# Attention and a feed-forward layer on one core: rows in parts of 256 and 320, and two PSUM banks used for more than one thing

## The chip, the cores and the metric

The kernel runs on 1 core of one Trainium2 chip. The metric is the device time of one execution in microseconds (us). Times of the kernel before: median 686.18 us of 3 runs (685.65 to 686.38). PE stands for TensorE, DVE for VectorE, ACT for ScalarE, SP for the engine that issues most DMAs.

## The reference

Shapes: 8 batches, 8 heads, 576 rows, head size 64, 32 memory slots, model width 512, inner width 2048, all in float32.

```python
a = exp(phi - max(phi, axis=2)); a = a / sum(a, axis=2)      # over the rows, per head
k_m = einsum('bhsm,bhsd->bhmd', a, k);  v_m = the same with v
scores = q @ k_m.T / sqrt(64);  attn = softmax(scores)       # over 32 memory slots
x = attn @ v_m                                               # 4608 x 512
out = silu(x @ w_in) @ w_out                                 # the feed-forward layer
```

The kernel never forms x: it multiplies v_m with w_in first (P, 256 x 2048 for a batch), and attn with P.

## The kernel before, in words

Every product that counts is made of parts: a float32 number is split into a high part, which a one-pass matmul takes as it is, and a low part, and three products (high x high, high x low, low x high) are summed.

A batch is a pass. Its 576 rows are held as two parts of 288: each is 256 rows and half of the 64 rows that are left over. The first layer (h = attn P, line 822 in passes 2 to 7, line 678 in batches 0 and 1) writes two PSUM banks, h, one tile of `[128, 2, 512]`, allocated anew each step. silu reads h (lines 836 and 838; 703 and 705 in batches 0 and 1): the 256 main rows go to gbuf, the 32 of the left-over rows to gleft.

A pass from 2 on has 16 steps (slots 0 to 15). In step s = 8 t + j PE first runs `ffn1s(b, t, j)`, 12 matmuls for the row half t and two chunks of 128 of the inner width; then `run(b, s)` puts in what the table of events holds for that step; then `st_step` of the step before, 21 matmuls of 256 columns into four banks sum 0 to 3 (line 861), which make the second layer in seven products in place of eight. For these, `forms` makes high and low parts of seven combinations: ACT rounds three (840), DVE makes four sums (841 to 845), ACT rounds these (850, the second rounding), DVE makes the low parts (851, 852). In steps 2 and 11 (4 and 11 in pass 2) DVE does the second rounding (847, 848) since ACT has an exponential to do, with a table load before and after it. Passes 1, 3, 5 and 7 end with four left steps (slots 16 to 19) for the left-over rows of two batches.

The work for batch n = b + 1 is put into pass b as events: `phi_max`, `phi_fold`, `phi_sub`, `phi_exp` (a); `e_mm` in two parts (k_m and v_m, lines 335 and 345), and behind its second part the division by the sums on DVE (353, 355) and the two normalised halves kvn on ACT (359) and DVE (361); `e_tr` (transposes); `s_all` (scores, line 382); then softmax; `s_back` and `s_low` (transposes back, copy ahi on ACT line 466, alo on DVE 471); and four blocks of P, `p_mm` (line 640): 16 small matmuls into the two banks bg, then ACT copies the high part (656) and DVE makes the low part (658). Block k (512 of the inner width) is needed by steps 2k, 2k + 1, 2k + 8 and 2k + 9 of its pass. A DVE instruction of an event other than P and s_all stands behind the last low part of the step's forms and of P.

The order on PE, and on ACT from batch 1 on, is that of the text. DVE's order is the scheduler's, except for such ties. bg, two banks, serves P, e, its transposes and the scores; the scores' last 64 columns go beside h, in columns from 288 on of its banks. A tile is emptied before PE writes it anew.

Of the kernel before, what the change touches and what calls it, by code (L numbers as in the profile page):

```python
# [48 lines left out]
def attn_ffn_kernel(  # L49
# [166 lines left out]
    def beside_h(w):  # L216

        return [live["h"][:, i, HALF : HALF + w] for i in range(2)]
# [24 lines left out]
    def load_q(b, hf, few=False):  # L243
        t = sb.tile([P, NR, HALF], F32, tag=f"q{hf}", name=f"q{b}_{hf}", bufs=1)
        at[b]["q", hf] = t
        load(t.rearrange("p r s -> p (r s)"), qT[b, hf], few)
# [78 lines left out]
    def e_mm(b, cs=range(FULLC)):  # L325
        e, er, kvt, kr = (at[b][k] for k in ("e", "er", "kv", "kr"))
        if cs[0] == 0:
            at[b]["pt"] = beside_h(KVW) if b == 2 else banks(b)
# [34 lines left out]
    def e_tr(b):  # L363
        pt = beside_h(P) if b <= 2 else banks(b)
# [7 lines left out]
    def s_all(b):  # L372

        sc = at[b]["sc"] = sb.tile([P, 2, S], F32, tag="x" if b == 2 else "y", name=f"sc{b}", bufs=1)
        bg, left = bgtile(), beside_h(S - 512)
        kvT = at[b]["kvT"]
        w = 512 - HALF
        for hf, f, n in ((0, 0, HALF), (1, 0, w), (1, w, HALF - w)):
            for r in range(NR):
                for p in range(2):  # L380
                    to = left[p] if f else bg[:, p, hf * HALF : hf * HALF + n]
# [4 lines left out]
                        start=True, stop=True, skip_group_check=True,  # L386
# [7 lines left out]
    def s_mm(b, hf):  # L394
# [56 lines left out]
    def s_back(b, u):  # L451
# [13 lines left out]
        for x in ((0, HALF), (HALF, S)) if b == 1 else ((0, w),):  # L465
# [33 lines left out]
    def f_scores(u):  # L499
        if u == 0:  # L500
            t = [ps.tile([P, 512], F32, tag="acc", name=f"firsts{p}", bufs=NI) for p in range(2)]
        else:
            h = ps.tile([P, 2, 512], F32, tag="h", name="firsts", bufs=1)
            t = [h[:, p] for p in range(2)]
        kvT, q = at[0]["kvT"], at[0]["q", u]
        for r in range(NR):
            for p in range(2):
                nc.tensor.matmul(
                    t[p][M * r : M * (r + 1), :HALF],
# [4 lines left out]
        first["st", u] = t if u == 0 else h  # L514

    def f_copy(u):
# [3 lines left out]
        left = first["left"].rearrange("p (g h f) -> p g h f", g=2, h=2)[:, :, u]  # L520
        st = first["st", u]
        if u:
            nc.scalar.copy(t, st[:, :, : 2 * P])
            nc.scalar.copy(left, st[:, :, 2 * P : HALF])
            return
        nc.scalar.copy(t[:, 0], st[0][:, : 2 * P])
        nc.vector.tensor_copy(t[:, 1], st[1][:, : 2 * P])
        for p in range(2):
            nc.scalar.copy(left[:, p], st[p][:, 2 * P : HALF])

    def f_turn(u):
# [3 lines left out]
        else:  # L535
            t = ps.tile([P, 2, 512], F32, tag="h", name="firstu", bufs=1).rearrange("p b f -> p (b f)")
# [48 lines left out]
    def f_back(u):  # L585
# [27 lines left out]
    ALL, FIRST, SECOND = (0, S), (0, HALF), (HALF, S)  # L613
# [49 lines left out]
    def ffn1(b, fc, h=None, low_last=False):  # L663
# [4 lines left out]
        if h is None:  # L668
            h = live["h"] = ps.tile([P, 2, 512], F32, tag="h", name="h", bufs=1)
# [161 lines left out]
    def forms(b, t, j, h):  # L831
# [3 lines left out]
        w = MAIN // 2  # L835
# [31 lines left out]
    sums, begun = [], set()  # L867
    HIGH, LOW = ((0, 0), (0, 1)), ((1, 0),)

    def st_step(b, t, j, part):  # L870
        if j == 0:
            sums[:] = [ps.tile([P, DMODEL], F32, tag="acc", name=f"sum{i}", bufs=NI) for i in range(4)]
# [9 lines left out]
        order = [(HIGH, todo), (LOW, todo)]  # L882
        if j == NP - 1:
# [77 lines left out]
    def steady(b, n):  # L961
# [26 lines left out]
        for k in range(2):  # L988
            ev(b, 13 + k, p_mm, n, k * JW, JW)
# [10 lines left out]
    for b in range(B):  # L1000
# [11 lines left out]
        else:  # L1012
            ev(b, 0, win_load, b, 3)
            ev(b, 0 if b > 2 else 1, p_mm, b, 2 * JW, JW)
# [4 lines left out]
            ev(b, 2, p_mm, b, 3 * JW, JW)  # L1019
# [58 lines left out]
    idle = ps.tile([P, 2, 512], F32, tag="h", name="idle", bufs=1)[:, 0]  # L1078
# [230 lines left out]
```

## Time and profile before

| | |
|---|---|
| profiled execution | 686.28 us |
| its span | 684.4 us |
| median of the runs | 686.18 us |
| PE busy | 673.4 us (98%) |
| DVE busy | 515.2 us (75%) |
| ACT busy | 368.0 us (54%) |
| granted clock | 1.000 (mean), 9 in each of 40 slices |
| first-layer matmuls of the passes | 1152 of 128x288 |

Busy times add up what an engine works on, and a matmul's row runs from its issue to its modelled end, so rows of PE overlap and the distance between starts tells what PE can do. In a timeline, a row's bracket is the idle time of the engine before it and what ended it.

### The profile page before, as it was taken

What the parts mean: (1) busy time and instruction counts of PE and PEld (TensorE: products, weight loads), DVE (VectorE), ACT (ScalarE), POOL (GpSimd) and SP (SyncE); (2) the same over time, 40 slices, a digit from 0 to 9 for tenths busy, and PEclk for the clock granted to TensorE, in tenths of its full rate; (3) what the DMA queues carried; (4) which work ended last, traced back from release to release, by engine and by line L of the source; (5) the groups of instructions that cost most, each with busy time, mean ns of one, the idle gap of its engine ahead of it and who ended that gap; (6) DMA issues with size and microseconds to landing.
All of it is one profiled execution on the core that took longest, in us unless ns stands there. A gap on an engine that the chain in (4) does not pass through costs nothing.

```text
span 684.4 us, 14813 instructions
## 1 busy us (share of the span) xinstructions
PE 673.4 (98%) x5932; PEld 595.5 (87%) x5932; DVE 515.2 (75%) x1085; ACT 368.0 (54%) x677; POOL 0.7 (0%) x6
## 2 busy tenths in 40 slices
PE   8999999999999999999999999999999999999997
PEld 3578777887889998899998999899989999889997
DVE  4897899788938588868876678786885668767653
ACT  3778684533625455654644546563653646554541
POOL 0000000000000000000000000000000000000000
PEclk9999999999999999999999999999999999999999
DMA  9988984224260462253420444235431204210001
GB/s 341 338 337 278 314 317 158 105 110 148 92 222 16 151 226 85 78 169 138 171 93 17 139 132 181 73 94 182 154 105 52 79 1 155 82 58 17 32 1 47
DMA packets 38228, 93.93 MB, mean 137 GB/s; under 512 B 4752, under 2 KB 22032, under 8 KB 34576
## 3 DMA queue, kind: packets, MB, share of 16 engines
q1 hardware_dynamic: 37136, 90.22, 38.0%
q10 hardware_dynamic: 1024, 2.77, 1.1%
q8 instruction: 47, 0.77, 0.4%
q14 instruction: 21, 0.17, 0.1%
HBM read 77.22 MB, written 15.73 MB: 136 GB/s over the span
## 4 chain that ended last, share of the span: by engine, by line
PE 77%; DVE 5%; ACT 2%; issue 1%; DMA 1%; SPq 0%; DVEq 0%; ACTq 0%
PE sum L861 32%; PE h L822 20%; PE acc L719 7%; PE lsum L861 5%; PE h L678 4%; PE bg L640 4%; PE accleft L719 2%; PE bg L335 1%; PE bg L382 1%; DMA fm<-fm 1%; ACT gbuf L836 1%; DVE gbuf L841 0%; DVE pm L658 0%; DVE sc L431 0%; DVE smx L427 0%
## 5 line engine op out<-in xcount | busy, mean ns | idle before, releaser
L822 PE MATMUL h<-aparts,pm 128*128 128x288 f32 x1152 | 168.8, 295 | 0.2 <-ACT gleft L838 0.2
L822 PEld LDWEIGHTS h<-aparts,pm 128*128 128x128 f32 x1152 | 157.0, 188 | 0.8 <-ACT gleft L838 0.5
L836 ACT ACTIVATE gbuf<-h 128x512 f32<-128x512 f32 x96 | 57.3, 596 | 122.5 <-PE h L822 120.5
L861 PE MATMUL sum<-wo_hi,aparts 128*128 128x256 f32 x384 | 103.9, 293 | 0.0
L861 PE MATMUL sum<-kept,aparts 128*128 128x256 f32 x576 | 100.1, 282 | 0.0
L861 PE MATMUL sum<-wo_lo,aparts 128*128 128x256 f32 x384 | 100.0, 282 | 0.0
L841 DVE TENSOR_TENSOR gbuf<-gbuf 128x256 f32<-128x256 f32 x96 | 40.5, 422 | 76.1 <-ACT gbuf L836 75.5
L861 PEld LDWEIGHTS sum<-wo_hi,aparts 128*128 128x128 f32 x384 | 72.7, 189 | 19.2 <-ACT gleft L838 16.7
L850 ACT ACTIVATE aparts<-gbuf 128x512 fp32r<-128x512 f32 x86 | 54.4, 633 | 65.2 <-DVE gbuf L845 65.2
L719 PE MATMUL acc<-wo_hi,gparts 128*128 128x512 f32 x256 | 86.5, 397 | 0.4 <-DVE gparts L695 0.3
L861 PEld LDWEIGHTS sum<-kept,aparts 128*128 128x128 f32 x576 | 82.5, 191 | 0.0
L852 DVE TENSOR_TENSOR gparts<-gbuf,aparts 128x512 fp32r<-128x512 f32 x86 | 59.5, 692 | 19.2 <-ACT aparts L850 19.2
L861 PE MATMUL sum<-wo_hi,gparts 128*128 128x256 f32 x384 | 73.2, 281 | 0.0
L861 PEld LDWEIGHTS sum<-wo_lo,aparts 128*128 128x128 f32 x384 | 73.1, 190 | 0.0
L861 PE MATMUL sum<-kept,gparts 128*128 128x256 f32 x288 | 65.5, 282 | 0.0
L719 PEld LDWEIGHTS acc<-wo_hi,gparts 128*128 128x128 f32 x256 | 47.7, 188 | 14.7 <-DVE gparts L695 1.8
L861 PEld LDWEIGHTS sum<-wo_hi,gparts 128*128 128x128 f32 x384 | 59.4, 190 | 0.0
L678 PEld LDWEIGHTS h<-aparts,pm 128*128 128x128 f32 x372 | 51.8, 188 | 6.7 <-issue 2.7
L678 PE MATMUL h<-aparts,pm 128*128 128x288 f32 x372 | 56.0, 299 | 0.5 <-ACT aparts L608 0.4
L719 PE MATMUL acc<-wo_lo,gparts 128*128 128x512 f32 x128 | 50.5, 394 | 0.8 <-DVE wo_lo L184 0.7
L840 ACT ACTIVATE aparts<-gbuf 128x384 fp32r<-128x384 f32 x96 | 50.4, 525 | 0.0
L861 PEld LDWEIGHTS sum<-kept,gparts 128*128 128x128 f32 x288 | 47.9, 190 | 0.0
(206 smaller groups left out, 986.3 us busy)
## 6 DMA issues: line engine op xcount, KB each, us to landing
win<-win_saved SPq DMA_DIRECT2D x24, 1024.0 KB, 4.9
kv<-in_kv SPq DMA_DIRECT2D x28, 516.0 KB, 4.7
q<-in_q SPq DMA_DIRECT2D x16, 576.0 KB, 5.4
raw<-in_w_in SPq DMA_DIRECT2D x14, 512.0 KB, 7.3
raw<-in_w_out SPq DMA_DIRECT2D x6, 1024.0 KB, 5.9
win_saved<-win SPq DMA_DIRECT2D x4, 1024.0 KB, 9.0
phi<-in_phi SPq DMA_DIRECT2D x7, 576.0 KB, 5.8
out<-oo SPq DMA_DIRECT2D x26, 128.0 KB, 1.8
```

What stands on the lines that cost most here:

```text
L335: nc.tensor.matmul(pt[p][M * r : M * (r + 1), :KVW], e[:, p, c, M * r : M * (r + 1)], kvt[c][:, p, r], start=c == 0, stop=False, skip_grou ...
L382: nc.tensor.matmul(to[M * r : M * (r + 1)], kvT[D * p : D * (p + 1), 0, r], at[b]["q", hf][D * p : D * (p + 1), r, f : f + n], start=True, ...
L640: nc.tensor.matmul(bg[M * r : M * (r + 1), p, :w].rearrange("p (k f) -> p k f", f=P), kvT[D * p : D * (p + 1), 1, r], src[D * p : D * (p + ...
L678: nc.tensor.matmul(h[:, hf, :HALF], wt[:, p, fs], a[:, p, hf * HALF : (hf + 1) * HALF], start=n[hf] == 0, stop=n[hf] == 5, skip_group_chec ...
L719: nc.tensor.matmul(acc[key], gt[:, cs], wt[:, fc], start=fc == 0 and n == 0, stop=fc == NFC - 1 and n == 2)
L822: nc.tensor.matmul(h[:, i, :HALF], wt[:, p, f : f + P], a[:, p], start=n == 0, stop=n == 5)
L836: nc.scalar.activation(gbuf[:, :MAIN].rearrange("p (i f) -> p i f", i=2), h[:, :, :w], AF.Silu)
L840: nc.scalar.activation(hi[:, :3], g[:, 1:4], AF.Copy)
L841: nc.vector.tensor_tensor(g[:, 4:6], g[:, :1].broadcast_to([P, 2, P]), g[:, 1:3], op=ALU.subtract)
L850: nc.scalar.activation(hi[:, 3:], g[:, 4:], AF.Copy)
L852: last_split.append(nc.vector.tensor_tensor(lo[:, 3:], g[:, 4:], hi[:, 3:], op=ALU.subtract))
L861: nc.tensor.matmul(sums[bank][:, place * Q : (place + 1) * Q], gt[:, k], wt, start=bank not in begun, stop=True, skip_group_check=True,)
```

## The change

The rows of a batch are held as parts of 256 and 320 rows; the 64 left-over rows are all in the second. h becomes two tiles of one bank each. In passes from 2 on they are allocated once: in the first half (steps 0 to 7) both chunks of 256 columns stand in h[0], and h[1] is free; in the second half each chunk of 320 columns has a bank. The four sums are also allocated once; each uses its whole bank but sum 3, which uses 256 of 512 columns. For n > 2, e's two halves go to h[1] and the free half of sum 3's bank; for n > 3 the transposes go to h[1], and the scores' left-over columns to h[1] and sum 3's bank. In some steps the three matmuls on sum 3 come last. e's DVE instructions in passes 3 and later are no longer tied behind the low parts.

Blocks of P: P(2) of a pass moves from step 0 to 3 (pass 2: 1 to 2), P(3) from step 2 to 5, pass 7 stays. So in passes 3 to 6 P(2) stands in front of e's first part and P(3) in front of its second. P(0) of the next batch moves from step 13 to 12 in pass 2; in passes 3 and 5 P(0) and P(1) move from steps 13 and 14 to slot 17, one behind the other, P(1) into h and P(0) into bg. silu reads bank by bank; in the head, the scores of the second part are copied by ACT and DVE, and turned into bg.

```diff
+CUT = MAIN // 2
+PART = ((0, CUT), (CUT, S))
+WIDE = S - CUT
...
     def e_mm(b, cs=range(FULLC)):
         if cs[0] == 0:
-            at[b]["pt"] = beside_h(KVW) if b == 2 else banks(b)
+            if b > 2:
+                at[b]["pt"] = spare_bank()[:, :KVW], accs()[3][:, Q : Q + KVW]
+            else:
+                at[b]["pt"] = beside_h(KVW) if b == 2 else banks(b)
...
     def e_tr(b):
-        pt = beside_h(P) if b <= 2 else banks(b)
+        if b > 3:
+            pt = [spare_bank()[:, k * P : (k + 1) * P] for k in range(2)]
+        else:
+            pt = beside_h(P) if b <= 2 else banks(b)
...
     def s_all(b):
-        bg, left = bgtile(), beside_h(S - 512)
+        bg = bgtile()
+        left = [spare_bank()[:, :LEFT], accs()[3][:, Q + KVW : Q + KVW + LEFT]] if b > 3 else beside_h(LEFT)
...
+    def p_pair(b):
+        one, two = live["h"], bgtile()
+        p_group(b, JW, JW, one)
+        p_group(b, 0, JW, [two[:, p] for p in range(2)])
+        hi, lo = pj[b, 1]
+        for p in range(2):
+            nc.scalar.activation(hi[:, p], one[p], AF.Copy)
+        for p in range(2):
+            nc.vector.tensor_tensor(lo[:, p], one[p], hi[:, p], op=ALU.subtract)
+        p_split(b, 0, JW, two)
...
     def f_copy(u):
-        if u:
-            nc.scalar.copy(t, st[:, :, : 2 * P])
-            nc.scalar.copy(left, st[:, :, 2 * P : HALF])
-            return
         nc.scalar.copy(t[:, 0], st[0][:, : 2 * P])
         nc.vector.tensor_copy(t[:, 1], st[1][:, : 2 * P])
-        for p in range(2):
-            nc.scalar.copy(left[:, p], st[p][:, 2 * P : HALF])
+        if u:
+            for p in range(2):
+                nc.scalar.copy(first["left"][:, p * LEFT : (p + 1) * LEFT], st[p][:, 2 * P : WIDE])
...
     def ffn1s(b, t, j):
-        h = live["h"] = ps.tile([P, 2, 512], F32, tag="h", name="h", bufs=1)
-        ahi, alo = (at[b][x][:, :, t * HALF : (t + 1) * HALF] for x in ("ahi", "alo"))
+        if "fixed" not in live:
+            live["fixed"] = live["h"] = htiles()
+        h = live["h"]
+        h = [h[i][:, :WIDE] if t else h[0][:, i * CUT : (i + 1) * CUT] for i in range(2)]
+        ahi, alo = (at[b][x][:, :, slice(*PART[t])] for x in ("ahi", "alo"))
...
     def forms(b, t, j, h):
-        nc.scalar.activation(gbuf[:, :MAIN].rearrange("p (i f) -> p i f", i=2), h[:, :, :w], AF.Silu)
-        o = b % 2 * LEFT + t * (LEFT // 2)
-        nc.scalar.activation(gleft[:, 2 * j : 2 * j + 2, o : o + LEFT // 2], h[:, :, w:HALF], AF.Silu)
+        if t == 0:
+            nc.scalar.activation(gbuf[:, :MAIN], h[0], AF.Silu)
+        for i in range(2 * t):
+            nc.scalar.activation(gbuf[:, i * CUT : (i + 1) * CUT], h[i][:, :CUT], AF.Silu)
+            nc.scalar.activation(gleft[:, 2 * j + i, o : o + LEFT], h[i][:, CUT:WIDE], AF.Silu)
...
     def st_step(b, t, j, part):
         order = [(HIGH, todo), (LOW, todo)]
+        if j == 0 or t == 0 and j in (4, 6):
+            order = [(HIGH, todo[:2] + todo[3:]), (LOW, todo[:2] + todo[3:]), (HIGH + LOW, todo[2:3])]
...
-        for k in range(2):
-            ev(b, 13 + k, p_mm, n, k * JW, JW)
+        if b % 2:
+            ev(b, NFC + 1, p_pair, n)
+        else:
+            for k in range(2):
+                ev(b, 14 if k else 12 if b == 2 else 13, p_mm, n, k * JW, JW)
...
-            ev(b, 0 if b > 2 else 1, p_mm, b, 2 * JW, JW)
+            ev(b, 0 if n == B else 3 if b > 2 else 2, p_mm, b, 2 * JW, JW)
...
-            ev(b, 2, p_mm, b, 3 * JW, JW)
+            ev(b, 2 if n == B else 5, p_mm, b, 3 * JW, JW)
...
-                if i.engine == DVE and fn not in (p_mm, s_all):
+                if i.engine == DVE and fn not in (p_mm, p_pair, s_all, *((e_mm,) if b > 2 else ())):
```

## Rows read from the trace of the kernel before

**Rows 1.** The page, busy us, share and instructions of each engine.
```profile
PE 673.4 (98%) x5932; PEld 595.5 (87%) x5932; DVE 515.2 (75%) x1085; ACT 368.0 (54%) x677; POOL 0.7 (0%) x6
```
**Rows 2.** The chain of waits, a plain step of pass 4: start us, us, what.
```profile
410.15 1.60 PE h L822 x12
411.75 2.50 PE sum L861 x21
```
**Rows 3.** Timeline of PE, first layer in steps 2 to 6 of pass 4: start us, us.
```profile
371.59 1.74 PE L822 MATMUL h<-aparts,pm 128*128 128x288 f32 x12
...
376.89 1.74 PE L822 MATMUL h<-aparts,pm 128*128 128x288 f32 x12
...
382.19 1.76 PE L822 MATMUL h<-aparts,pm 128*128 128x288 f32 x12
...
386.30 1.75 PE L822 MATMUL h<-aparts,pm 128*128 128x288 f32 x12
...
391.97 1.76 PE L822 MATMUL h<-aparts,pm 128*128 128x288 f32 x12
```
**Rows 4.** Timeline of PE, step 14 of pass 2.
```profile
268.17 1.09 PE L640 MATMUL bg<-win,kvT 64*32 64x512 f32 x16 [1.02 <-DVE pm L658]
```
**Rows 5.** Timelines of PE and ACT, steps 5 and 6 of pass 2.
```profile
222.09 1.75 PE L822 MATMUL h<-aparts,pm 128*128 128x288 f32 x12
...
227.45 1.86 PE L822 MATMUL h<-aparts,pm 128*128 128x288 f32 x12
...
228.42 0.63 ACT L850 ACTIVATE aparts<-gbuf 128x512 fp32r<-128x512 f32 x1 [0.59 <-DVE gbuf L845]
```
**Rows 6.** Timeline of DVE, head, behind the first part's subtraction.
```profile
18.41 0.82 DVE L562 TENSOR_REDUCE fmx<-firstu 128x20 f32<-128x640 f32 x1 [0.85 <-PE firstu L542]
```
**Rows 7.** Timeline of PE, batch 1, where e follows a block of P.
```profile
133.13 1.09 PE L640 MATMUL bg<-win,kvT 64*32 64x512 f32 x16
134.16 1.97 PE L335 MATMUL h<-kv,phi 128*32 128x129 f32 x64
```
**Rows 8.** Timeline of all engines, step 0 of pass 3 with P.
```profile
277.69 0.60 ACT L836 ACTIVATE gbuf<-h 128x512 f32<-128x512 f32 x1 [1.05 <-PE h L822]
...
279.97 1.01 ACT L656 ACTIVATE pm<-bg 128x1024 fp32r<-128x1024 f32 x1
...
281.02 1.23 DVE L658 TENSOR_TENSOR pm<-bg,pm 128x1024 fp32r<-128x1024 f32 x1 [0.22 <-ACT pm L656]
...
281.21 0.95 PE L822 MATMUL h<-aparts,pm 128*128 128x288 f32 x6
```
**Rows 9.** Timeline of ACT, steps 2 and 3 of pass 4.
```profile
373.37 0.60 ACT L836 ACTIVATE gbuf<-h 128x512 f32<-128x512 f32 x1 [1.69 <-PE h L822]
...
374.46 1.03 ACT L656 ACTIVATE pm<-bg 128x1024 fp32r<-128x1024 f32 x1
...
379.28 0.60 ACT L836 ACTIVATE gbuf<-h 128x512 f32<-128x512 f32 x1
```
**Rows 10.** Timelines of ACT and DVE, steps 4 and 5 of pass 4.
```profile
383.99 0.60 ACT L836 ACTIVATE gbuf<-h 128x512 f32<-128x512 f32 x1 [2.33 <-PE h L822]
...
388.46 0.58 ACT L836 ACTIVATE gbuf<-h 128x512 f32<-128x512 f32 x1
...
390.36 0.63 ACT L850 ACTIVATE aparts<-gbuf 128x512 fp32r<-128x512 f32 x1 [0.77 <-DVE gbuf L845]
...
392.48 0.35 DVE L361 TENSOR_SCALAR kvn<-bg,rs 128x128 f32<-128x128 f32 x1 [0.43 <-ACT kvn L359]
```
**Rows 11.** Timeline of all engines, step 7 of pass 4, the scores' left-over columns.
```profile
398.90 0.19 PEld L382 LDWEIGHTS h<-q,kvT 64*32 64x32 f32 x16 [0.26 <-ACT gleft L838]
...
401.16 0.37 DVE L388 STREAM_TRANSPOSE sc<-h 128x64 f32<-128x64 f32 x2
```
**Rows 12.** Timelines of DVE and PE, step 7 of pass 2 and the next.
```profile
237.30 0.35 DVE L361 TENSOR_SCALAR kvn<-bg,rs 128x128 f32<-128x128 f32 x1 [0.43 <-ACT kvn L359]
...
237.33 0.96 PE L822 MATMUL h<-aparts,pm 128*128 128x288 f32 x6
```

More of the change, by code (lines that the diff above doesn't have):

```diff
@@ L216, in beside_h, with spare_bank, htiles @@
     def beside_h(w):
-        return [live["h"][:, i, HALF : HALF + w] for i in range(2)]
+        return [live["h"][i][:, WIDE : WIDE + w] for i in range(2)]
+    def spare_bank():
+        return live["h"][1]
+    def htiles(name="h"):
+        return [ps.tile([P, 512], F32, tag="h", name=f"{name}{i}", bufs=2) for i in range(2)]
     def load_phi(b):
@@ L243, in load_q @@
     def load_q(b, hf, few=False):
-        t = sb.tile([P, NR, HALF], F32, tag=f"q{hf}", name=f"q{b}_{hf}", bufs=1)
+        lo, hi = PART[hf]
+        t = sb.tile([P, NR, hi - lo], F32, tag=f"q{hf}", name=f"q{b}_{hf}", bufs=1)
         at[b]["q", hf] = t
-        load(t.rearrange("p r s -> p (r s)"), qT[b, hf], few)
+        load(t.rearrange("p r s -> p (r s)"), qT[b, :, NR * lo : NR * hi], few)
     def rows(p):
@@ L338, in e_mm @@
                     kvt[c][:, p, r],
-                    start=c == 0, stop=False, skip_group_check=True,
+                    start=c == 0 and (b < 3 or p == 0), stop=False, skip_group_check=True,
                 )
@@ L385, in s_all @@
                         at[b]["q", hf][D * p : D * (p + 1), r, f : f + n],
-                        start=True, stop=True, skip_group_check=True,
+                        start=not f or b < 4 or p == 0, stop=True, skip_group_check=True,
                     )
@@ L502, in f_scores @@
         else:
-            h = ps.tile([P, 2, 512], F32, tag="h", name="firsts", bufs=1)
-            t = [h[:, p] for p in range(2)]
+            t = htiles("firsts")
         kvT, q = at[0]["kvT"], at[0]["q", u]
@@ L513, in f_scores @@
                 )
-        first["st", u] = t if u == 0 else h
+        first["st", u] = t
     def f_copy(u):
@@ L633, in p_mm, with p_group @@
     def p_mm(b, f, w, low=True):
+        bg = bgtile()
+        p_group(b, f, w, [bg[:, p] for p in range(2)])
+        if low:
+            p_split(b, f, w, bg)
+        return bg
+    def p_group(b, f, w, bg):
         j = f // JW
         src = wins[b, j] if b > 1 else win[j]
-        bg = bgtile()
         kvT = at[b]["kvT"]
@@ L702, in silu @@
         w = MAIN // 2
-        nc.scalar.activation(g32.rearrange("p (h f) -> p h f", h=2), h[:, :, :w], AF.Silu)
+        for hf in range(2):
+            nc.scalar.activation(g32[:, hf * w : (hf + 1) * w], h[hf][:, :w], AF.Silu)
         o = b % 2 * LEFT
         i = nc.scalar.activation(
-            gleft[:, fc, o : o + LEFT].rearrange("p (h f) -> p h f", h=2), h[:, :, w:HALF], AF.Silu
+            gleft[:, fc, o : o + LEFT], h[1][:, w:WIDE], AF.Silu
         )
@@ L867, in attn_ffn_kernel, with accs @@
     sums, begun = [], set()
+    def accs():
+        if not sums:
+            t = [ps.tile([P, DMODEL], F32, tag="acc", name=f"sum{i}", bufs=NI) for i in (3, 0, 1, 2)]
+            sums[:] = t[1:] + t[:1]
+        return sums
     HIGH, LOW = ((0, 0), (0, 1)), ((1, 0),)
@@ L871, in st_step @@
         if j == 0:
-            sums[:] = [ps.tile([P, DMODEL], F32, tag="acc", name=f"sum{i}", bufs=NI) for i in range(4)]
+            accs()
             begun.clear()
@@ L1155, in attn_ffn_kernel @@
         split(g32, steps=(1,), gs=gs)
-        g32 = silu(0, 1, ffn1(0, 1, bgtile()))
+        bg = bgtile()
+        g32 = silu(0, 1, ffn1(0, 1, [bg[:, p] for p in range(2)]))
         w_conv(I1, None, "a")
@@ L1200, in run @@
         todo = events.pop((b, slot), [])
-        todo.sort(key=lambda e: e[0] is not p_mm)
+        todo.sort(key=lambda e: e[0] not in (p_mm, p_pair))
         last_p.clear()
@@ L1285, in layout @@
     )
[L1286 to L1291 removed]
+    qT = q.reshape(B, NR, 2, S, D).transpose(0, 2, 4, 1, 3).reshape(B, P, NR, S)
+    qT = np.concatenate([qT[..., lo:hi].reshape(B, P, -1) for lo, hi in PART], axis=2)
     return {
```

48 lines of the change are left out of this document (18 added, 30 removed).

## The prediction

> **What bounds the kernel now.** I read the page's busy times first, then the chain of waits, then timelines of single steps. The page has PE busy 98% of the span, DVE 75%, ACT 54% [rows 1], and the granted clock is full speed in every slice. So time can come only from what PE runs, or from the few places where it stands. A plain step of a pass is 12 first-layer matmuls in 1.60 us and 21 second-layer ones in 2.50 us, 4.10 us, without a gap [rows 2]. The steps of pass 4 are longer where something is slipped in: 5.30 us with a block of P (step 2), 5.30 with e's first part (step 3), 5.67 with its second part (step 5) [rows 3]. So a block of P costs 1.20 us, and e 1.20 and 1.57. Beside this the reader sees one real stand of PE in the passes, 1.02 us in pass 2, where a second block of P waits for DVE to empty bg [rows 4], and one of 0.16 us ahead of and in its step 6, which starts 5.36 us after step 5 in place of 5.30 and takes 1.86 in place of 1.76 [rows 3, 5].
>
> **Parts of 256 and 320 rows.** A matmul takes 2.50/21 = 0.119 us at 256 columns and 1.60/12 = 0.133 at 288 [rows 2], 0.44 ns a column; at 320 no row exists, and the straight line gives 0.147 (0.145 to 0.150). The first half's 12 matmuls become 0.17 us shorter and the second half's 0.17 longer: nothing in sum (-0.3 to +0.6 us over 96 steps and two main batches). But steps 0 to 7 of a pass last 3.93 us now, with the same work on ACT and DVE. ACT gets two 256-wide silus and two 64-wide ones in the second half's steps, one instruction and no 64-wide one in the first half's; it is free 46% of the time [rows 1], and each bank is read as soon as its own six matmuls end: nothing. In the head one more DVE copy stands ahead of the subtraction; DVE idles 0.85 us there [rows 6]: nothing (-0.3 to +0.4). The q loads are 4 and 5 KB a partition in place of 4.6 each, on the same queue with as many issues; they are long landed: nothing.
>
> **Fewer switches: the gain.** In pass 1 e already stands right behind P: it starts 1.03 us after P [rows 7], while P alone lengthens its step by 1.20. So 0.17 us goes in entering and leaving a block, and is saved where two stand together. P blocks and e parts in a pass now stand in the steps 0, 2, 3, 5, 13, 14 (pass 2: 1, 2, 5, 7, 13, 14); afterwards in 3, 5 and 17 (passes 3 and 5), 3, 5, 13, 14 (4 and 6), 2, 5, 7, 12, 14 (2). That is 3 + 3 + 2 + 2 + 1 = 11 switches, 1.9 us (1.1 to 2.2). The Trainium skill (TensorEngine Tiling (Array Packing), Key Properties) says that changing the tiling mode drains TensorE, and gives no price; with the 128 cycles of drain of its TensorE: Matmul & The Clock Gate, Single matmul latency, an estimate is 0.05 us a change, 1.2 us for 22 changes, and the time below would be 0.7 us higher. No row here separates the drain from the rest of the 0.17.
> P in steps 12 and 14 of pass 2 takes away its 1.02 us [rows 4], since bg has a whole step more; the 0.16 us goes too, as P stands in front of the waiting matmul. Gain 1.9 + 1.02 + 0.16 = 3.1 us.
>
> **What is late then: step 3 of passes 3 to 6.** The moved block P(2) was made four steps ahead of its use; now it is made in step 3 for step 4, and P(3) in step 5 for step 6. Behind a step's own silu, ACT takes the P block only after the step's second rounding, so its low part on DVE ends 281.02 + 1.23 - 277.69 = 4.56 us after that silu's start, while the next step's matmuls start 3.52 us after it [rows 8]. With e behind P that becomes 3.52 + 1.03 = 4.55, and the low part is wanted by the fifth matmul, at 5.03. On time, if silu is. But silu of step 3 stands behind the exponential: it starts 5.91 us after that of step 2, of which 1.03 was P's copy that moves away [rows 9]; 4.88 against the 3.93 of PE is 0.95 late. P's low part is ready at 5.5: PE stands 0.5 us (0 if silu were on time; 0.9 if DVE puts other work first).
>
> **Step 5 of passes 3 to 6.** Silu of step 5 starts 4.47 us after that of step 4, behind the copy of ahi; against 3.93 it is 0.54 late. ACT's second rounding ends 2.53 after silu [rows 10] and the P copy 0.93 later (1.01 less the overlap), 4.0 from silu's own time. Only then come e's two normalised halves, one on ACT and, behind it, one on DVE, 0.43 + 0.35 [rows 10]: 4.78 at the earliest. One of e's halves now lies in the free columns of sum 3's bank. Does PE wait for a reader of other columns of a bank? Here it does: the scores' leftover columns in h were held until ACT had read h's silu columns [rows 11]. So the three matmuls on sum 3, put last in this step, wait for DVE. PE would be there at 391.97 - 388.09 + 1.03 - 0.36 = 4.55 after silu's own time (388.09 is 383.99 + 4.10; the step's end [rows 3], P, three matmuls). If DVE takes e's half first, PE stands 0.25, and then 0.3 more for P's low part; if it takes P's low part first, which is ready 0.4 earlier, 1.0; if e's reciprocals come behind that too, 1.9. Nothing orders e's work in these passes, so I take the one that is ready first: 1.0 (0.3 to 1.9). Step 7: the last leftover columns are also in sum 3's bank, and DVE takes them out just ahead of the next step [rows 11], and sum 3's turn is 0.36 us before that: 0.1 (0 to 0.3).
> Together 1.6 us a pass, 6.4 for four.
>
> **Pass 2.** Its exponential is in step 4 and holds silu of step 5 back; that step's second rounding ends at 229.05 [rows 5], long after its matmuls. P(3), now in this step, is copied by 230.0 and split by 231.25. Step 6 would start at 227.39 + 1.03 = 228.4: it stands 1.6 for the high part, and at its fifth matmul 0.75 for the low one: 2.35 (1.8 to 3.0, as PE gains 0.5 on the way there, and DVE gets rid of a P block in step 1). In step 7 e's half is ready at 237.65, and sum 3's turn is 0.36 ahead of 237.33 [rows 12]: 0.7 (0 to 0.9). Sum 3.05.
>
> **The other moves.** Two blocks of P in step 17 of passes 3 and 5 have two more left steps until use, and h is idle there; their four copies lie beside other work: nothing. Each window of weights is read later than before, and its buffer's next load comes in step 14 or later: no DMA is held, and SP's queue has the same entries. Sums in fixed banks: the first step of a half takes sum 3 last, after DVE has emptied it: nothing.
>
> **The sum.** 6.4 + 3.05 - 3.1 = +6.35, that is 692.6. The profiled execution took 686.28 us (span 684.4), 0.1 above the median of the runs, 686.18: 692.5 against the median.
>
> **Rivals.** (1) Faster: the waits are covered. It decides where silu of step 3 is less than 0.45 late and DVE takes e first with P's copy 0.3 earlier; for it speaks that PE has no such stand in 684 us now, against it the rows of steps 3 and 5, whose lateness is measured. Then 686.2 - 3.1 = 683.1. (2) No change: only pass 2 pays, 686.2 + 3.05 - 3.1 = 686.1. For it: its delay of silu is by far the longest. Against: it needs four passes without any wait. (3) Much slower: DVE takes e's reciprocals last, four times 1.9 in place of 1.0 and 0.9 in step 3: 692.5 + 4 x 1.3 = 697.7. For it speaks that e is traced behind P; against it that e's columns are ready over a microsecond before. (4) A reader in one half of sum 3's bank does not hold PE in the other: then step 5 loses its 1.0 (P's low part, first on DVE, is ready at 5.27, and wanted at 3.88 + 1.03 + 0.48 = 5.39), both steps 7 too: 692.5 - 4 x 1.1 - 0.7 = 687.4. Against it stand [rows 11].
>
> **Chances.** The forecast 0.50, its own range 688 to 697; (1) 0.23, (2) 0.12, (3) 0.09, (4) 0.06. A measurement of this kernel can tell about 0.2%, 1.4 us, from no change, so (4) goes with (2): faster 0.23, no change 0.18, slower 0.59. The range 683.2 to 697 leaves out half of (1) and most of (3).
>
> **What would show it.** PE rows of the first layer in steps 4 and 6 with a wait for DVE's P split (L658's successor) of 0.3 to 1 us, eight times; matmuls on sum 3 waiting for kvn in step 5; in pass 2 a wait of 1.6 us for ACT's P copy ahead of step 6; no L640 wait at the end of pass 2; P and e rows without the 0.17 between. It is wrong if PE's waits in the passes stay under 1 us in sum, or if the second half's 320-column matmuls take other than 0.147.

## The result, and the profile after

The changed kernel takes 695.29 us (median of 4 runs, 694.54 to 695.48), the kernel before 686.17 (685.65 to 686.38): ratio 1.0132, 95% interval 1.0114 to 1.015. It is slower by 9.1 us; 6.35 was forecast, with the sign right and the time inside the range. The page of the changed kernel gives busy us, share and instructions of each engine, the answer to [rows 1]:

```profile
PE 674.0 (97%) x5932; PEld 598.7 (86%) x5932; DVE 517.6 (75%) x1088; ACT 382.1 (55%) x758; POOL 0.7 (0%) x6
```

PE has as many instructions as before and is busy 0.6 us longer, in a span that is 9.2 us longer (693.6). So PE runs the same instructions and stands more. Two of the page's costliest groups say where (busy, mean ns of one, idle before, what ended most of it):

```profile
L852 PE MATMUL h<-aparts,pm 128*128 128x256 f32 (+1 forms) x1152 | 171.3, 297 | 4.4 <-DVE pm L684 2.5
...
L894 PE MATMUL sum<-kept,aparts 128*128 128x256 f32 x576 | 101.0, 284 | 5.6 <-DVE kvn L374 5.1
```

The same groups on the page of the kernel before stand next to nothing:

```profile
L822 PE MATMUL h<-aparts,pm 128*128 128x288 f32 x1152 | 168.8, 295 | 0.2 <-ACT gleft L838 0.2
...
L861 PE MATMUL sum<-kept,aparts 128*128 128x256 f32 x576 | 100.1, 282 | 0.0
```

In the changed kernel the first layer (L852) waits for P's low part (and in pass 2 for its high part), the matmuls on sum 3 (among L894) for e's normalised half. The timeline of PE, first layer in steps 2 to 6 of pass 4, answers [rows 3]:

```profile
373.13 1.60 PE L852 MATMUL h<-aparts,pm 128*128 128x256 f32 x12
...
377.07 1.59 PE L852 MATMUL h<-aparts,pm 128*128 128x256 f32 x12
...
383.23 0.72 PE L852 MATMUL h<-aparts,pm 128*128 128x256 f32 x4
...
384.47 1.22 PE L852 MATMUL h<-aparts,pm 128*128 128x256 f32 x8 [0.52 <-DVE pm L684]
...
388.04 1.57 PE L852 MATMUL h<-aparts,pm 128*128 128x256 f32 x12
...
396.07 1.57 PE L852 MATMUL h<-aparts,pm 128*128 128x256 f32 x12
```

From start to start, the steps of pass 4 took in us:

| step | 0 | 1 | 2 | 3 | 4 | 5 | 6 | 7 |
|---|---|---|---|---|---|---|---|---|
| before | 5.66 | 4.07 | 5.29 | 5.30 | 4.11 | 5.67 | 4.31 | 5.51 |
| after | 4.31 | 3.93 | 3.94 | 6.17 | 4.81 | 8.02 | 4.13 | 5.59 |

A plain step of the first half is 3.93 as forecast. Steps 0 and 2 lose P's 1.20 each, step 3 takes it up for 1.02 (6.17 less 5.30, plus the 0.15 by which such a step is shorter now). Step 4 is 0.88 over a plain step, step 5 is 1.49 over its sum (3.93 + 1.57 for e + 1.03 for P). The second half's steps, by the chain of waits, answer [rows 2] with 320 columns: 1.77 and 2.52, 4.28 from start to start.

```profile
405.95 1.77 PE h L852 x12
407.71 2.52 PE sum L894 x21
```

By the starts of the passes in both traces (198.97, 275.91, 361.87, 437.38, 523.53, 598.71 and the end at 680.87 before; 197.44, 276.72, 364.89, 442.34, 530.48, 607.93 and 690.06 after), the difference is made up so (the forecast's parts add up to 6.40, since its sum took the 1.87 of the switches as 1.9):

| | batches 0, 1 | pass 2 | 3 | 4 | 5 | 6 | 7 | sum |
|---|---|---|---|---|---|---|---|---|
| forecast | 0 | +1.70 | +1.09 | +1.26 | +1.09 | +1.26 | 0 | +6.40 |
| measured | -1.53 | +2.34 | +2.21 | +1.94 | +1.99 | +2.27 | -0.03 | +9.19 |

**Step 3 to 4.** The timeline of ACT in steps 2 and 3 of pass 4 answers [rows 9]:

```profile
374.76 0.60 ACT L868 ACTIVATE gbuf<-h 128x512 f32<-128x512 f32 x1 [1.56 <-PE h L852]
...
378.58 1.28 ACT L868 ACT_TABLE_LOAD   x1 [0.19 <-DVE gparts L881]
379.88 0.60 ACT L868 ACTIVATE gbuf<-h 128x512 f32<-128x512 f32 x1
...
382.15 1.01 ACT L682 ACTIVATE pm<-bg 128x1024 fp32r<-128x1024 f32 x1
```

silu of step 3 starts 5.12 after that of step 2 (4.88 forecast): the table load ahead of it waits 0.19 for DVE's low part of step 2. From silu to the end of P's low part it is 4.53 (384.41 less 379.88), where 4.56 was forecast; PE's fifth matmul starts at 384.47. Timeline of DVE:

```profile
383.19 1.22 DVE L684 TENSOR_TENSOR pm<-bg,pm 128x1024 fp32r<-128x1024 f32 x1 [0.22 <-ACT pm L682]
```

In pass 3 silu of step 3 starts 5.43 after that of step 2, and PE waits 0.30 for P's high part too, ahead of step 4: step 3 takes 6.47 there.

**Step 5.** The timeline of DVE, pass 4:

```profile
393.57 0.15 DVE L366 TENSOR_SCALAR rs<-h 128x1 f32<-128x1 f32 x1
393.64 0.15 DVE L366 TENSOR_SCALAR rs<-sum 128x1 f32<-128x1 f32 x1
393.75 0.16 DVE L368 RECIPROCAL rs<-rs 128x1 f32<-128x1 f32 x1
393.87 1.23 DVE L684 TENSOR_TENSOR pm<-bg,pm 128x1024 fp32r<-128x1024 f32 x1
395.01 0.15 DVE L368 RECIPROCAL rs<-rs 128x1 f32<-128x1 f32 x1
395.20 0.35 DVE L374 TENSOR_SCALAR kvn<-sum,rs 128x128 f32<-128x128 f32 x1
```

P's low part stands between e's two reciprocals. The second of them, 0.15 us of work, is what e's half in sum 3's bank needs, and it came 1.2 late by that. PE had been at sum 3's matmuls at 394.20 (timeline of PE):

```profile
393.96 0.40 PE L894 MATMUL sum<-kept,gparts 128*128 128x256 f32 x2
395.61 0.51 PE L894 MATMUL sum<-kept,aparts 128*128 128x256 f32 x2 [1.24 <-DVE kvn L374]
```

**Pass 2.** PE stands 1.9 us for P's high part and 0.7 for its low one. And the granted clock falls. The windows (us; busy us and instructions of PE, PEld, DVE, ACT, POOL; granted clock; DMA share; GB/s) of the changed kernel:

```profile
224.70:226.70 2.00, 0.28 (x3) 0.08 (x1) 1.54 (x4) 1.54 (x2) 0.00 (x0) 1.00 0.74 301
226.70:227.70 1.00, 0.88 (x4) 0.58 (x4) 0.98 (x1) 0.00 (x0) 0.00 (x0) 0.74 0.00 0
227.70:228.70 1.00, 0.70 (x3) 0.70 (x4) 0.25 (x1) 0.00 (x0) 0.00 (x0) 0.50 0.00 0
228.70:229.70 1.00, 1.00 (x7) 1.00 (x7) 0.00 (x0) 0.00 (x0) 0.00 (x0) 0.50 0.06 16
```

```profile
226.74 0.88 PE L852 MATMUL h<-aparts,pm 128*128 128x256 f32 x4 [1.76 <-ACT pm L682]
228.00 2.08 PE L852 MATMUL h<-aparts,pm 128*128 128x256 f32 x8 [0.38 <-DVE pm L684]
```

0.50 is 1.2 GHz, the lower of the two levels: matmuls of 256 columns follow each other by 0.21 us there in place of 0.12. By the 0.74 of the second window it fell at 227.2: PE had stood for 1.9 us, had gone on at 226.74 and was at the last of the four matmuls. The second stand came behind the fall.

### The profile page after: what moved, and what is told of

The parts are those of the page before. It is cut to its first block, busy times and chain, and to the rows that moved or that the text cites. A ratio compares the mean times of both kernels' runs of the same rounds, so it can differ in the third digit from the quotient of the medians.

```text
span 693.6 us, 14807 instructions
## 1 busy us (share of the span) xinstructions
PE 674.0 (97%) x5932; PEld 598.7 (86%) x5932; DVE 517.6 (75%) x1088; ACT 382.1 (55%) x758; POOL 0.7 (0%) x6
## 4 chain that ended last, share of the span: by engine, by line
PE 62%; DVE 15%; ACT 6%; issue 3%; DMA 0%; SPq 0%; DVEq 0%; ACTq 0%
PE sum L894 29%; PE h L852 18%; PE acc L746 7%; PE h L704 4%; PE bg L657 2%; ACT aparts L883 2%; DVE gbuf L874 2%; DVE pm L684 2%; PE accleft L746 2%; ACT gbuf L868 1%; DVE gbuf L877 1%; DVE gbuf L878 1%; ACT pm L682 1%; DVE gparts L885 1%; DVE aT L481 1%
## 5 line engine op out<-in xcount | busy, mean ns | idle before, releaser
L852 PE MATMUL h<-aparts,pm 128*128 128x256 f32 (+1 forms) x1152 | 171.3, 297 | 4.4 <-DVE pm L684 2.5
L852 PEld LDWEIGHTS h<-aparts,pm 128*128 128x128 f32 x1152 | 158.3, 190 | 6.2 <-DVE pm L684 3.6
L894 PE MATMUL sum<-wo_hi,aparts 128*128 128x256 f32 x480 | 120.6, 290 | 0.0
L894 PE MATMUL sum<-wo_lo,aparts 128*128 128x256 f32 x432 | 112.9, 283 | 0.0
L874 DVE TENSOR_TENSOR gbuf<-gbuf 128x256 f32<-128x256 f32 x96 | 40.6, 423 | 88.5 <-ACT gbuf L868 59.0
L894 PE MATMUL sum<-kept,aparts 128*128 128x256 f32 x576 | 101.0, 284 | 5.6 <-DVE kvn L374 5.1
L894 PEld LDWEIGHTS sum<-wo_hi,aparts 128*128 128x128 f32 x480 | 88.5, 191 | 11.7 <-ACT gleft L871 4.2
L894 PEld LDWEIGHTS sum<-kept,aparts 128*128 128x128 f32 x576 | 82.4, 191 | 7.5 <-DVE kvn L374 6.2
L894 PE MATMUL sum<-wo_hi,gparts 128*128 128x256 f32 x480 | 88.3, 283 | 0.0
L894 PEld LDWEIGHTS sum<-wo_lo,aparts 128*128 128x128 f32 x432 | 82.6, 191 | 0.0
L894 PEld LDWEIGHTS sum<-wo_hi,gparts 128*128 128x128 f32 x480 | 73.0, 191 | 0.0
L870 ACT ACTIVATE gbuf<-h 128x256 f32<-128x256 f32 x96 | 36.9, 384 | 55.7 <-PE h L852 55.5
L868 ACT ACTIVATE gbuf<-h 128x512 f32<-128x512 f32 x48 | 28.6, 596 | 70.3 <-PE h L852 70.3
L894 PE MATMUL sum<-kept,gparts 128*128 128x256 f32 x288 | 65.6, 282 | 0.0
L704 PE MATMUL h<-aparts,pm 128*128 128x256 f32 (+1 forms) x372 | 56.0, 299 | 1.2 <-ACT aparts L619 0.6
```

Source lines behind the costliest of these rows:

```text
L704: nc.tensor.matmul(h[hf][:, : PART[hf][1] - PART[hf][0]], wt[:, p, fs], a[:, p, slice(*PART[hf])], start=n[hf] == 0, stop=n[hf] == 5, skip ...
L852: nc.tensor.matmul(h[i], wt[:, p, f : f + P], a[:, p], start=n == 0, stop=n == 5, skip_group_check=True,)
L868: nc.scalar.activation(gbuf[:, :MAIN], h[0], AF.Silu)
L870: nc.scalar.activation(gbuf[:, i * CUT : (i + 1) * CUT], h[i][:, :CUT], AF.Silu)
L874: nc.vector.tensor_tensor(g[:, 4:6], g[:, :1].broadcast_to([P, 2, P]), g[:, 1:3], op=ALU.subtract)
L894: nc.tensor.matmul(sums[bank][:, place * Q : (place + 1) * Q], gt[:, k], wt, start=bank not in begun, stop=True, skip_group_check=True,)
```

## Experiments

All kernels compute the whole reference. The sum of the parts is read from the starts of the steps in the profiled execution, the time is the median.

**P back in its old steps.** Is step 5's stand owed to e's place in sum 3's bank, or to P beside it?

```diff
-ev(b, 0 if n == B else 3 if b > 2 else 2, p_mm, b, 2 * JW, JW)
+ev(b, 0 if b > 2 else 1, p_mm, b, 2 * JW, JW)
-ev(b, 2 if n == B else 5, p_mm, b, 3 * JW, JW)
+ev(b, 2, p_mm, b, 3 * JW, JW)
```

> The changed kernel (695.3) with P(2) and P(3) back where they were: steps 0 and 2 in passes 3 to 6, 1 and 2 in pass 2. Theory A, that P's low part is late for step 4 and that sum 3 waits for e's half in its bank, whatever P does: step 4's stand of 0.85 goes, two switches of 0.17 a pass come back, pass 2 loses its 4.3 of stands and slow clock; step 5 loses P on PE (1.03) and on DVE alike, so its sum 3 stands some 1.4 as now. About 689. Rival B, that step 5's stand comes from P in that step alone: it goes as well, four times 1.4, about 683.

684.55 us (684.3 to 684.92, 10 runs); the ratio to the kernel before is 0.9979, its interval 0.9969 to 0.9988. That is rival B's side (about 683, where A had 689), and a little faster than both kernels. Step 4 is plain again (3.93), and step 5 takes 5.67 to 5.73, which is 0.2 over its sum (3.93 + 1.57): 1.3 of the 1.49 went with P. My bookkeeping for theory A was wrong: a block of P adds 1.03 to PE, but its copy on ACT (1.01) and then its low part on DVE (1.23) both stand ahead of e's half. Without P, DVE also took e's sums ahead of the low parts of the step's forms. Timeline of DVE, step 5 of pass 4 of this kernel:

```profile
386.98 0.15 DVE L366 TENSOR_SCALAR rs<-h 128x1 f32<-128x1 f32 x1
387.05 0.15 DVE L366 TENSOR_SCALAR rs<-sum 128x1 f32<-128x1 f32 x1
387.12 0.28 DVE L878 TENSOR_TENSOR gbuf<-gbuf 128x128 f32<-128x128 f32 x1
...
387.79 0.22 DVE L368 RECIPROCAL rs<-rs 128x1 f32<-128x1 f32 x2
388.04 0.35 DVE L374 TENSOR_SCALAR kvn<-sum,rs 128x128 f32<-128x128 f32 x1
```

e's half is finished 5.2 us after the step's start (383.18); in the changed kernel it is 7.5 (388.04 to 395.55).

**e's halves swapped.** Which reader of the bank does PE wait for?

```diff
-at[b]["pt"] = spare_bank()[:, :KVW], accs()[3][:, Q : Q + KVW]
+at[b]["pt"] = accs()[3][:, Q : Q + KVW], spare_bank()[:, :KVW]
-start=c == 0 and (b < 3 or p == 0)
+start=c == 0 and (b < 3 or p == 1)
```

> The changed kernel with e's two halves swapped in passes 3 and later: the half that ACT normalises, first, lies in sum 3's bank, and the one that DVE normalises in the free bank. Theory A, that PE's matmuls on sum 3 wait for the reader of the other columns of their bank: ACT's half ends 1.17 before DVE's, so the stand in step 5 falls from 1.41 to 0.25, four times: about 690.7. Rival C, that what PE waits for is P's low part or DVE's queue as such: the stand only moves into step 6's fifth matmul, and the time stays within 1 us of 695.3.

690.57 (689.79 to 692.37); 1.0071, interval 1.0054 to 1.0088: theory A. Step 5 becomes 6.85 in each of the four passes, 1.17 less, and step 6 stays as it was. Timelines of ACT and of PE, pass 4 of this kernel:

```profile
393.43 0.37 ACT L372 ACTIVATE kvn<-sum,rs 128x128 f32<-128x128 f32 x1 [0.17 <-DVE rs L368]
```

```profile
393.85 0.50 PE L894 MATMUL sum<-kept,aparts 128*128 128x256 f32 x2
```

PE goes on 0.05 after ACT has read the bank's other columns (393.43 + 0.37), while DVE's half, in another bank now, is still to come (timeline of DVE):

```profile
394.62 0.35 DVE L374 TENSOR_SCALAR kvn<-h,rs 128x128 f32<-128x128 f32 x1
```

So in this program a reader of 129 columns holds matmuls on other columns of the same bank. The Trainium skill (PSUM — Partial Sum Buffer, PSUM bank collisions raise a hardware error) says to guard PSUM by bank and group of 32 partitions, or simply by bank, and not by address; by that a program that goes by the rule waits whenever it puts a reader beside a sum, and the trace agrees.

**DVE takes e first.** The forecast had several prices for step 5, by DVE's order. Here P's low part is put behind e's normalised half.

```diff
+            if fn is p_mm and slot == 5 and 2 < b < B - 1:
+                live["bg"] = p_mm(*a, low=False)
+                p_split(*a, live["bg"], (0,))
+                late = a
+                continue
             fn(*a)
+            if fn is e_mm and slot == 5 and 2 < b < B - 1:
...
+                i = nc.vector.tensor_tensor(lo[:, :, c], bg[:, :, : late[2]], hi[:, :, c], op=ALU.subtract)
+                behind(i.ins, last_kvn[-1])
```

> The changed kernel with DVE's order in step 5 of passes 3 to 6 altered: P's low part comes behind e's normalised half, in place of between its two reciprocals. Theory A: e's half is ready at 394.8 in place of 395.55 of the changed kernel's pass 4, so sum 3 stands 0.65 in place of 1.41; P's low part is later by 0.9 and holds the fifth matmul of step 6 for 0.3: gain 0.5 a pass, about 693.3. Rival C, that ACT's P copy or P's low part bounds the step: no gain or a loss, 695 to 697.

692.43 (691.88 to 692.62); 1.0093, interval 1.0078 to 1.0109: theory A, with 0.86 a pass in the trace where I had given it 0.5. Timeline of DVE, pass 4 of this kernel (L1260 is P's low part):

```profile
392.60 0.15 DVE L366 TENSOR_SCALAR rs<-h 128x1 f32<-128x1 f32 x1
392.67 0.15 DVE L366 TENSOR_SCALAR rs<-sum 128x1 f32<-128x1 f32 x1
392.79 0.23 DVE L368 RECIPROCAL rs<-rs 128x1 f32<-128x1 f32 x2
393.05 0.35 DVE L374 TENSOR_SCALAR kvn<-sum,rs 128x128 f32<-128x128 f32 x1
393.32 1.22 DVE L1260 TENSOR_TENSOR pm<-bg,pm 128x1024 fp32r<-128x1024 f32 x1
```

From [rows 10] I had read that DVE's half waits for ACT's. It does not, both start at 393.05; it waits for its own reciprocal. Step 5 falls by 1.19 and step 6 grows by 0.33 in each pass: the prediction's first case, a stand of 0.25 and then 0.3 for P's low part.

**Pass 2 alone.** P(2) and P(3) go back to steps 1 and 2 in pass 2 only.

```diff
-ev(b, 0 if n == B else 3 if b > 2 else 2, p_mm, b, 2 * JW, JW)
+ev(b, 0 if n == B else 3 if b > 2 else 1, p_mm, b, 2 * JW, JW)
-ev(b, 2 if n == B else 5, p_mm, b, 3 * JW, JW)
+ev(b, 5 if 2 < b < B - 1 else 2, p_mm, b, 3 * JW, JW)
```

> The changed kernel with only pass 2's P(2) and P(3) back in steps 1 and 2. Theory A: the stands of 1.9 and 0.8 ahead of and in step 6 go, and with them the stretch at half clock that follows them (1.2 us more), less one switch of 0.17: 4.0 less, about 691.3, and a granted clock of 1.0 throughout. Rival D, that the slow clock there is not a consequence of the stand: 2.6 less, 692.7.

692.48 (692.43 to 692.9); 1.0095, interval 1.0078 to 1.0112. By the time alone it looks like rival D (692.7; A had 691.3), but the clock is 1.00 through steps 4 to 8 now. Pass 2 is 3.14 shorter: the stands and the half clock together were 3.87 over plain matmuls; 0.49 came back as waits in steps 4 and 5, and 0.17 as a switch. In the profiled execution pass 2 also starts 0.5 later than in the changed kernel's, by when the first loads landed (PE waits 0.57 for one of k and v), which hides some more. So A's price of 4.0 was too high by the waits and the switch that come back with P in its old steps. Whether the fall of the clock follows from the stand is told by the next run.

**P(2) alone back in passes 3 to 6.**

```diff
-ev(b, 0 if n == B else 3 if b > 2 else 2, p_mm, b, 2 * JW, JW)
+ev(b, 0 if b > 2 else 2, p_mm, b, 2 * JW, JW)
```

> The changed kernel (695.29) with only P(2) back in step 0, in passes 3 to 6; P(3) stays in step 5 with e's second part. Theory A, that the stands of steps 4 and 5 add up, since step 4's own silu and so all that step 5 waits for moves forward with PE: each pass gains step 4's 0.88 less a switch of 0.19, and pass 3 0.3 more: 3.1, about 692.2. Rival E, that step 5's end is set by a chain on ACT and DVE that PE's stand in step 4 doesn't delay: what step 4 gains is given back in step 5, and the time is 695 to 696.

693.55 (691.78 to 693.74); 1.0112, interval 1.0095 to 1.0129. The time lies between the two theories (692.2; 695 to 696), so the trace decides. Passes 4 and 6 gain 0.7 each and pass 5 0.85; step 4 is plain again (3.93), and step 5 stays at 8.02 (8.16 in pass 5): A, the two stands add up. In pass 3 step 4 gains as well, but step 5 grows by 0.81, since DVE's order came out another way (timeline of DVE, pass 3 of this kernel):

```profile
304.34 0.23 DVE L368 RECIPROCAL rs<-rs 128x1 f32<-128x1 f32 x2
304.49 1.22 DVE L684 TENSOR_TENSOR pm<-bg,pm 128x1024 fp32r<-128x1024 f32 x1
305.63 0.34 DVE L374 TENSOR_SCALAR kvn<-sum,rs 128x128 f32<-128x128 f32 x1
```

PE stands 2.2 there, more than the 1.9 that the prediction gave the worst order. This profile also tells of the clock. Its pass 2 has the same two stands, in the same place (windows as above):

```profile
224.60:226.70 2.10, 0.33 (x3) 0.12 (x2) 1.62 (x5) 1.54 (x2) 0.00 (x0) 1.00 0.76 311
226.70:227.70 1.00, 0.74 (x4) 0.54 (x4) 1.00 (x1) 0.00 (x0) 0.00 (x0) 1.00 0.01 4
227.70:228.70 1.00, 0.74 (x6) 0.74 (x7) 0.21 (x1) 0.00 (x0) 0.00 (x0) 1.00 0.00 0
```

Here the clock did not fall, and step 6 took 4.81 in place of 5.95. So the fall costs 1.14 us, and it does not follow from the stand alone. The profile is of the fastest execution of this kernel, 691.78 us, with a mean granted clock of 1.000; the other three, of 693.46 to 693.74, have 0.998. The changed kernel's executions are alike: 1.000 in the one of 694.54 us, 0.998 in those of 695.19, 695.39 and 695.48. The Trainium skill (TensorE: Matmul & The Clock Gate, What's actually happening) says that what the clock gate looks at runs freely and is not tied to the kernel, so that one kernel can differ from run to run; the executions of these two kernels agree.

**Towards a better version.** Three kernels start from P in its old steps. The first puts e, its transposes and the ties of its DVE work back as in the kernel before. The second and third have e's halves swapped, as above, and move P(3) to step 3, in front of e's first part, and s_norm to step 2: the second in passes 3 to 6, the third in 4 and 6 alone. The edits are shown against the kernel with P in its old steps, that of the third against the second.

```diff
-at[b]["pt"] = spare_bank()[:, :KVW], accs()[3][:, Q : Q + KVW]
+at[b]["pt"] = banks(b)
...
-if i.engine == DVE and fn not in (p_mm, p_pair, s_all, *((e_mm,) if b > 2 else ())):
+if i.engine == DVE and fn not in (p_mm, p_pair, s_all):
```

> The kernel with P(2) and P(3) back in their old steps (684.55 in the first series), and e's halves and transposes back in bg as well, with DVE's work for e tied behind the low parts again; only the scores' left-over columns still use sum 3's bank. In that earlier kernel step 5 still stands 0.2 a pass on sum 3 and pass 2's step 7 0.4. If e's place in sum 3's bank is what costs there: 1.2 less, 683.4. If it costs nothing without P beside it, 684.5. More than 685.5 would mean that the old place of e has a price of its own.

684.60 (684.18 to 684.94, 11 runs); 0.998, interval 0.9972 to 0.9989: no difference to 684.55. Step 5 is 0.2 shorter in each pass and step 7 of pass 2 0.43, but step 3 is longer by 0.85 in pass 3 and 0.24 in pass 5: e's first part starts 0.1 after DVE has read P(3) out of bg (289.87 in pass 3). Either place of e has its price.

```diff
-ev(b, 2, p_mm, b, 3 * JW, JW)
+ev(b, 3 if 2 < b < B - 1 else 2, p_mm, b, 3 * JW, JW)
-ev(b, 3, s_norm, b, SECOND)
+ev(b, 2, s_norm, b, SECOND)
...
-left = [spare_bank()[:, :LEFT], accs()[3][:, Q + KVW : Q + KVW + LEFT]]
+left = [accs()[3][:, Q + KVW : Q + KVW + LEFT], spare_bank()[:, :LEFT]]
```

> What the runs so far point to: P(2) in step 0 and P(3) in step 3, in front of e's first part, two steps ahead of its use (steps 1 and 2 in pass 2); the half of e that ACT normalises, and the scores' columns that DVE turns first, in sum 3's bank; DVE's s_norm in step 2 and not in step 3. Against P(2) and P(3) in their old steps (684.55): one switch a pass, 0.7; step 5's stand, 0.8; step 7's, 0.6; about 682.5. If P's low part in step 3 holds back step 5's silu, each pass stands 0.5 more than that: 684.5.

684.86 (684.65 to 685.2, 11 runs); 0.9984, interval 0.9975 to 0.9993: a miss, 682.5 was expected. The switch is saved in each pass (steps 2 and 3 together 0.19 shorter) and step 7 gains 0.13, but step 5 keeps its 0.2 in passes 4 and 6 and grows by 1.24 in pass 3 and 0.28 in pass 5. Timeline of DVE, pass 3 of this kernel:

```profile
294.28 1.23 DVE L684 TENSOR_TENSOR pm<-bg,pm 128x1024 fp32r<-128x1024 f32 x1 [0.22 <-ACT pm L682]
295.42 1.21 DVE L944 TENSOR_TENSOR x<-x,oo 128x256 f32<-128x256 f32 x3
296.55 0.42 DVE L874 TENSOR_TENSOR gbuf<-gbuf 128x256 f32<-128x256 f32 x1
```

Three additions of the second layer's output come behind P's low part, and step 4's sums (L874) after them. But in pass 5 the same three stand in the same place, and step 5 grows by 0.28 only. What pass 3 has besides is a later silu of step 3: the table load ahead of it waits longer for DVE's low part of step 2 (timelines of ACT, pass 3 and pass 5 of this kernel), and silu starts 7.95 after step 2 does, in place of 7.01.

```profile
289.66 1.28 ACT L868 ACT_TABLE_LOAD   x1 [1.38 <-DVE gparts L881]
...
451.03 1.28 ACT L868 ACT_TABLE_LOAD   x1 [0.44 <-DVE gparts L881]
```

```diff
-ev(b, 3 if 2 < b < B - 1 else 2, p_mm, b, 3 * JW, JW)
+ev(b, 3 if b in (4, 6) else 2, p_mm, b, 3 * JW, JW)
-ev(b, 2, s_norm, b, SECOND)
+ev(b, 3 if b % 2 else 2, s_norm, b, SECOND)
```

> The version of the run before with its P(3) in step 3 and s_norm in step 2 only in passes 4 and 6; in passes 3 and 5 they stand in steps 2 and 3, since there DVE has three more additions for the second layer's output in step 3 (1.2 us), which came behind P's low part and held step 4's forms, and step 5 stood 1.2 and 0.3. If that is the cause, both go: against P(2) and P(3) in their old steps (684.55) two switches of 0.19 and four times 0.13 in step 7 are left, about 683.7. If the wait in pass 3 has another cause, 684.5 or more.

684.40 (684.19 to 687.14, 12 runs); 0.9981, interval 0.9972 to 0.9989; 683.7 was expected. The long stand of pass 3 is gone. That does not show the additions as its cause, as the edit puts both P(3) and s_norm back in passes 3 and 5; step 5 of passes 3 and 5 is still 0.2 longer than in the kernel these versions start from. The intervals of these versions overlap: what they share, P(2) in step 0 and P(3) no later than step 3, is what beats both kernels, and nothing here tells the rest apart. In the trace of the first of them (P back in its old steps) the gain over the kernel before does not lie in passes 3 to 7, which are 0.5 longer: it is 1.6 by the start of pass 2 and 0.8 in pass 2.

**The first batches.** The last two kernels are the kernel before with edits of the head; the second has the first one's edit too.

```diff
-t = ps.tile([P, 2, 512], F32, tag="h", name="firstu", bufs=1).rearrange("p b f -> p (b f)")
+t = bgtile().rearrange("p b f -> p (b f)")
```

> The kernel before with one line changed: in the head, the second part's scores are turned into bg and not into a tile of h, so that PE need not wait until h's columns are copied out. The changed kernel reaches pass 2 1.5 earlier than the kernel before, which no step of the prediction has. If this edit is the cause: 1.0 less, 685.1. If the causes are the other edits of the two first batches, or how early the first loads land: no change, 686.1.

685.98 (685.43 to 686.14, 11 runs) against 685.95; 0.9998, interval 0.9989 to 1.0007: no change. In the trace the stretch from the first transposes to the second layer is 0.15 shorter (16.56).

```diff
-nc.scalar.copy(t, st[:, :, : 2 * P])
+nc.scalar.copy(t[:, 0], st[:, 0, : 2 * P])
+nc.vector.tensor_copy(t[:, 1], st[:, 1, : 2 * P])
```

> The kernel before with the second part's scores turned into bg, and their copy out of h split between ACT and DVE, as the changed kernel does. Read from the trace, from the first transposes (13.35 in the kernel before) to the first matmul of the second layer: 16.72 before, 16.56 with bg alone, 16.24 in the changed kernel. If the split copy is the rest: 16.25. If not: 16.5. The time itself moves by 0.5 at most, 685.6.

Missed: 16.69 for that stretch, where 16.25 or 16.5 was expected (687.32 us in a single run, whose first transposes start 0.8 later than in the kernel before). The split copy is not the rest, at least with h as one tile of two banks.

## Why the prediction was right, and where its sizes were off

- **Parts of 256 and 320: right.** Pass 7, where P isn't moved, is 0.03 shorter. A matmul of 320 columns follows by 0.147, one of 256 by 0.118; steps 0 to 7 are 0.14 to 0.19 shorter than before, steps 8 to 15 0.14 to 0.18 longer.
- **Fewer switches: right.** A block of P that leaves a step takes 1.20 with it and costs 1.02 in front of e. The estimate from the Trainium skill's drain (TensorEngine Tiling (Array Packing), Key Properties, with TensorE: Matmul & The Clock Gate, Single matmul latency), 0.10 for a change there and back, is below the 0.18 of these rows. It took the 128 cycles at 2.4 GHz; the Trainium skill has them in its sum for 1.2 GHz, and at that clock the estimate would be 0.21, a little above. The pair in step 17 costs 2.08 where two steps lost 2.42: timeline of PE, pass 3.

```profile
354.28 1.09 PE L657 MATMUL h<-win,kvT 64*32 64x512 f32 x16
355.16 1.06 PE L657 MATMUL bg<-win,kvT 64*32 64x512 f32 x16
356.15 0.39 PE L894 MATMUL sum<-wo_hi,aparts 128*128 128x256 f32 x1
```

- **Pass 2's wait of 1.02 [rows 4]: right,** it is gone; step 14 takes 5.48 in place of 6.40.
- **Step 3 to 4: mechanism right, 0.5 forecast, 0.88 measured.** silu was 0.24 later than taken, behind DVE: PE stands 0.68. The other 0.2 it loses in starting twice, at the step's first matmul and behind the stand: the next matmul follows by 0.20 and 0.23 in place of 0.12. Pass 3 has 0.30 more, for P's high part.
- **Step 5: mechanism right, 1.0 forecast, 1.49 measured.** The order that DVE took lay between the two that I priced at 1.0 and 1.9. Swapping the halves took 1.2 of it away, and so did taking e first (where step 6 took back 0.33); P out of the step took 1.3: it needs both, P beside e and e in the sum's bank. The sign that was named for step 6, a wait of the first layer for P's low part, is not there in these passes, since DVE took that part ahead of e's half.
- **Step 7: 0.1 forecast, 0.25 measured** in passes 3, 4 and 6, and 0.5 in pass 5.
- **Pass 2, step 5 to 6: 2.35 forecast, about 3.9 measured,** of which 1.14 is the clock, a term that the forecast did not have. Step 7 took 0.45 (0.7 forecast).
- **Head and first batches: "nothing" forecast, -1.53 measured.** Nine profiles have the changed kernel's head; their first transposes start at 12.73 to 13.40 (12.90 in the changed kernel), those of the kernel before at 13.35. So 0.45 of the gain lies ahead of them, in when the loads land, and that alone differs by up to 0.7 among these profiles. From there to the second layer it is 16.25 in all nine against 16.71, and from there to the last matmul into acc 159.9 against 160.5. Of these 1.1 us the turn into bg explains 0.15; the rest stays open.
- **Rivals.** (1) and (2) fall: four passes wait as measured. (4) falls with the swapped halves. (3) named the right danger, DVE's order, and pass 3 of one experiment shows it.

So 6.35 was too low by 3.7 over passes 3 to 6 (the terms of steps 4, 5 and 7) and by 0.6 in pass 2, and too high by the 1.5 of the first batches. That it was no further off is in part luck: without these 1.5 the time would have been 696.8, just inside the range. In pass 2 the clock and the longer stands, 1.5 over their forecast, were partly met by step 9, which got 0.31 shorter where the longer part alone makes it 0.17 longer, and by step 7; at the end of pass 4 a stand of 0.34 went that the forecast had not counted.

## What to carry to other kernels

When a block of work is put beside another to save a switch on the busiest engine, follow what the block does on the other engines before the neighbour's reader: here 1.03 on PE brought 2.2 us on ACT and DVE, and a saving of 0.18 cost 1.5. A free half of a bank isn't free while the other half is being written: put there the half whose reader comes first, and fix that reader's place in its engine's order. And give a moved step as many steps of lead as it had, most of all around an exponential.

## What was not expected of the hardware

The granted clock fell to 1.2 GHz for some 3 us after PE had stood for 1.9 us in pass 2. In the changed kernel's trace it fell 0.45 us after PE had gone on, ahead of the second stand; with e's halves swapped 2.3 us after, behind both stands; with P(2) back in passes 3 to 6 not at all, though PE stood alike. It cost 1.14 us. Stands of 1.4 us in four passes of the same trace did not do so.
